# Attention scores from heads in place: two query tiles at once on halves or quarters of TensorE's array, without the moves that stacked high and low parts

## The chip, the cores and the metric

The kernel runs on one core of a Trainium2 chip. The core has five engines with queues of their own: TensorE (PE; its weight loads are shown apart as PEld), VectorE (DVE), ScalarE (ACT), GpSimd (POOL) and SyncE (SP), which here only issues DMAs. The metric is the device time of one execution in microseconds (us). Before the change the median of three runs is 1133.67 us (1133.57 to 1135.0); the execution that was profiled took 1130.16 us, and its profile spans 1128.2 us.

## The reference

Attention with a threshold, then a two-layer network with a quadratic gate:

```python
# q, k, v: 8 batches x 8 heads x 576 positions x 64, float32
scores = (1 / sqrt(64)) * q @ k^T
thresh = max(scores, axis=-1) - tau                  # tau = 0.02
scores = where(scores >= thresh, scores, -1e9)
attn = exp(scores - max(scores)); attn /= sum(attn) + 1e-9
x = (attn @ v), heads side by side                   # 4608 tokens x 512
h = x @ w_in                                         # 512 x 2048
g = where(h >= 1, h, where(h <= -1, 0, (h + 1)**2 / 4))
out = g @ w_out                                      # 2048 x 512
```

## The kernel before

**Numbers in two halves.** To keep nearly float32 precision on TensorE, every operand is scaled by a power of two and split into an fp16 high part and an fp16 low part (the rest). A product is made as high x high + low x high + high x low.

**Tiling.** The heads of a batch are taken as four pairs. A pair's q and k come from memory with the head dimension first, as 128 partitions: head 0 on partitions 0 to 63, head 1 on 64 to 127, 576 columns each. The queries of a pair are cut into two parts (256 and 320 positions; in batch 0 into three of 128, 128 and 320). A part consists of *tiles* of 128 query rows against all 576 keys. A full tile belongs to one head. The 320 positions leave 64 over for each head, and these make one *mixed* tile with head 0's rows on partitions 0 to 63 of the result and head 1's on 64 to 127. There are 288 tiles, 36 of them in batch 0.

**Scores.** A tile's scores go into one of two PSUM buffers `s` (two banks each, one for each half of the 576 keys). In batch 0 a full tile takes six matmuls on half of the array's rows (64 partitions of q and k, three products, two halves of the keys). In the batches after it the fp16 parts are first rearranged: ACT and DVE or POOL write them into `nat` (`hi` and `lo` in `add_qk`), and eight DMAs a pair (`move`, lines 591 to 596) copy them into `qq`, where a head's high part lies on partitions 0 to 63 and its low part on 64 to 127, and into `kk`, where each part of k lies on both halves. Then one matmul over 128 partitions makes (high + low) of q times one part of k, and a full tile takes four matmuls of 288 columns on the whole array. A mixed tile takes eight on half of its columns, two at a time.

**After the scores** (`add_tile`): DVE scales them and takes each row's minimum of the negated scores (`smax`, L994, and the threshold `sthr`, L998); ACT takes the exponential (`sexp`, L1001); DVE masks and sums (`smask`, L1015), which is the last reader of the buffer `s`; POOL normalizes (L1033), ACT and POOL split (L1038, L1041) into `hl`; SP sends it through a transposing DMA (L1063) into one of two buffers `eT`. When all tiles of a part are there, `add_av` multiplies with the transposed v (`av`, L1141, 28 matmuls on half of the columns each). Its result goes as high and low parts into `x`.

**The network.** For 256 tokens at a time, `ffn1` (L1213) makes 512 columns of h in `ph` with 24 or 48 matmuls; ACT and DVE apply the gate (L1219 to L1236); `ffn2` (L1258) adds to `acc`, 6 matmuls a step. The float64 weights are loaded, converted and split in the first 150 us.

**What sets the order.** The program is a list of operations (`plan.op`, with engine, planned duration, predecessors, buffers to take). A table of numbers, `ORDER`, gives the sequence in which `Plan.order` starts them; it gives each a planned time from the planned durations, `HOP` (handover between engines), `FREE`, `QUEUE`, `TURN` (PE's change between array shapes, told by an operation's `mode`), and each engine's instructions are issued sorted by it. Nothing is reordered at run time: each engine works through its list and waits where an operand or a buffer isn't ready. `take` names the rings of buffers: `s` (2), `ph` (3), `eT` (2), `hl` (3), `nat` (2), `kk` and `qq` (4 each).

Of the kernel before, what the change touches and what calls it, by code (L numbers as in the profile page):

```python
# [1319 lines left out]
```

## Time and profile before

| | |
|---|---|
| median of 3 runs | 1133.67 us |
| profiled execution | 1130.16 us |
| its span | 1128.2 us |
| mean granted TensorE clock | 0.987 |
| share of the 16 DMA engines taken by packets | 76.5% |
| share of the chain that ended last on PE | 70% |

A row of the timeline or of the groups gives the engine, the line, the operation, what it writes and reads, the part of the array that a matmul uses (`64*128` is 64 rows by 128 columns of the array), the shape of the moving operand, and how many. The ends of matmuls are modelled, so that neighbours overlap on paper; the time that a group really takes of PE is the start of the next row less its own, where nothing is noted as idle between.

### The profile page before, as it was taken

How to read it: one execution, taken by the hardware profiler on the slowest of the kernel's cores; microseconds unless marked ns; L12 is line 12 of the kernel's file. 1: busy time of each engine (PE TensorE's matmuls, PEld its weight loads, DVE VectorE, ACT ScalarE, POOL GpSimd, SP SyncE). 2: the span in 40 equal slices, each digit the busy share in tenths (PEclk: the TensorE clock that was granted, in tenths of full speed). 3: DMA queues.
4: the chain of work that ended last, by engine and by line, in shares of the span. 5: the costliest groups of instructions: out<-in, count | busy, mean ns of one | idle time of the engine just before them, and what ended most of it. 6: DMA issues, size and time to landing. Idle time of an engine off the chain costs nothing.

```text
span 1128.2 us, 26977 instructions
## 1 busy us (share of the span) xinstructions
PE 1088.4 (96%) x9396; PEld 756.9 (67%) x9396; DVE 892.0 (79%) x2704; ACT 868.7 (77%) x1676; POOL 790.2 (70%) x904
## 2 busy tenths in 40 slices
PE   4799999999999999999999999999999999999998
PEld 3456657766677676776777677676767677676674
DVE  5999889889689888899879898797679888785231
ACT  7989768779778788878877789777879877686352
POOL 6999997667766898678865986767787875655000
PEclk9799999999999999999999999999999999999999
DMA  9896899878968999669946999759796887554000
GB/s 332 345 208 143 148 207 189 145 142 185 206 125 148 200 193 228 135 134 198 216 96 114 182 203 195 122 106 200 163 197 140 171 157 133 105 103 97 19 11 20
DMA packets 435929, 179.40 MB, mean 159 GB/s; under 512 B 400464, under 2 KB 407632, under 8 KB 435792
## 3 DMA queue, kind: packets, MB, share of 16 engines
q1 hardware_dynamic: 435792, 177.67, 76.5%
q8 instruction: 74, 1.21, 0.4%
q14 instruction: 63, 0.52, 0.1%
HBM read 45.09 MB, written 9.44 MB: 48 GB/s over the span
## 4 chain that ended last, share of the span: by engine, by line
PE 70%; POOL 9%; DVE 8%; ACT 4%; DMA 4%; issue 4%; SPq 1%; DVEq 0%; POOLq 0%; ACTq 0%
PE acc L1258 27%; PE ph L1213 26%; PE s L977 9%; PE ph L1141 7%; POOL hl L1041 3%; DMA eT<-hl 2%; DVE s L994 2%; POOL e L1033 2%; DVE e L1015 2%; ACT e L1001 1%; DMA kk<-nat 1%; ACT hl L1038 1%; DMA WO<-in_moe_w_in_dram 1%; POOL raw L564 1%; SPq L594 0%
## 5 line engine op out<-in xcount | busy, mean ns | idle before, releaser
L1041 POOL TENSOR_TENSOR hl<-e,hl 128x576 f16<-128x576 f32 x285 | 366.6, 1292 | 115.8 <-ACT hl L1038 109.7
L1213 PE MATMUL ph<-x,WI 128*128 128x256 f16 (+1 forms) x4032 | 398.9, 257 | 1.5 <-DVE x L1153 0.7
L1213 PEld LDWEIGHTS <-WI 128*128 128x128 f16 x4032 | 346.3, 98 | 49.7 <-issue 5.8
L1033 POOL TENSOR_SCALAR e<-e,sm 128x576 f32<-128x576 f32 x285 | 219.1, 773 | 95.8 <-DVE sm L1025 62.2
L994 DVE TENSOR_SCALAR_CACHE_REDUCE s<-s,pc 128x576 f32<-128x576 f32 x288 | 232.7, 819 | 62.3 <-PE s L977 61.4
L1001 ACT ACTIVATE e<-s,sm 128x576 f32<-128x576 f32 x288 | 211.5, 741 | 62.5 <-DVE s L994 39.7
L1015 DVE SCALAR_TENSOR_TENSOR e<-s,sm,e 128x578 f32<-128x578 f32 x285 | 230.4, 815 | 33.1 <-ACT e L1001 28.6
L1038 ACT ACTIVATE hl<-e 128x576 f16<-128x576 f32 x285 | 193.1, 682 | 52.3 <-POOL e L1033 37.6
L1258 PE MATMUL acc<-WO,ga 128*128 128x512 f16 x864 | 202.3, 379 | 0.0
L977 PE MATMUL s<-kk,qq 128*128 128x288 f16 (+3 forms) x1360 | 190.5, 289 | 9.1 <-DVE e L1015 3.4
L977 PEld LDWEIGHTS <-qq 128*128 128x128 f16 (+3 forms) x1360 | 112.9, 100 | 71.8 <-issue 32.0
L1226 DVE SCALAR_TENSOR_TENSOR ph<-ph,fcs,asq 128x512 f32<-128x512 f32 (+1 forms) x160 | 112.0, 701 | 60.3 <-ACT asq L1222 59.1
L1219 ACT ACTIVATE asq<-ph,fcs 128x512 f32<-128x512 f32 (+1 forms) x160 | 115.6, 734 | 51.7 <-PE ph L1213 50.9
L1258 PEld LDWEIGHTS <-ga 128*128 128x128 f16 x864 | 82.5, 98 | 86.1 <-issue 2.4
L1141 PE MATMUL ph<-eT,vst 128*64 128x320 f16 (+2 forms) x1928 | 125.7, 282 | 7.5 <-DMA eT<-hl 2.3
L1141 PEld LDWEIGHTS <-vst 128*64 128x64 f16 x1928 | 100.8, 111 | 30.5 <-issue 20.5
L1236 DVE SCALAR_TENSOR_TENSOR ga<-ph,fcs,ga 128x256 f16<-128x256 f32 (+1 forms) x160 | 70.8, 451 | 29.7 <-ACT gb L1231 13.6
L1222 ACT ACTIVATE asq<-asq 128x512 f32<-128x512 f32 x144 | 90.8, 630 | 2.1
L1231 ACT ACTIVATE ga<-ph,fcs 128x256 f16<-128x256 f32 (+1 forms) x160 | 70.3, 451 | 27.8 <-DVE ph L1226 24.8
L1258 PE MATMUL acc<-WO,gb 128*128 128x512 f16 x300 | 72.8, 379 | 0.0
L1258 PE MATMUL acc<-WO,WI 128*128 128x512 f16 x288 | 67.2, 379 | 0.0
L1258 PE MATMUL acc<-WO 128*128 128x512 f16 x276 | 66.9, 379 | 0.0
(183 smaller groups left out, 1119.3 us busy)
## 6 DMA issues: line engine op xcount, KB each, us to landing
kk<-nat SPq DMA_DIRECT2D x112, 144.0 KB, 3.1
raw<-in_v_dram SPq DMA_DIRECT2D x32, 288.0 KB, 4.0
raw<-in_q_dram SPq DMA_DIRECT2D x32, 288.0 KB, 3.9
raw<-in_k_dram SPq DMA_DIRECT2D x32, 288.0 KB, 3.9
...
qq<-nat SPq DMA_DIRECT2D x112, 72.0 KB, 2.3
...
```

The costliest lines, as they stand in the source:

```text
L977: T.matmul(ap(s, s_ps)[r, f, :SH], q, k, start=ql == kl == 0, stop=kl == 1)
L994: V.tensor_scalar(sv(), sv(), c[:, 24 + v : 25 + v], None, ALU.mult, ALU.min, accum_out=t[:, 0:1])
L1001: A.activation(ev(), sv(), AF.Exp, bias=ap(m, sm)[:, 0:1], scale=-1.0)
L1015: V.scalar_tensor_tensor(ev(SH + 1), sv(SH + 1), t[:, 2:3], ev(SH + 1), ALU.is_le, ALU.mult, accum_out=t[:, 3:4])
L1033: G.tensor_scalar(ev(), ev(), ap(m, sm)[:, 5:6], ESC, ALU.mult, ALU.mult)
L1038: A.activation(part2(0), ev(), AF.Copy)
L1041: G.tensor_tensor(part2(w), ev(), part2(0), ALU.subtract)
L1141: T.matmul(o[hd * D : (hd + 1) * D, :n], vt[:, k, hd * D : (hd + 1) * D], t[:, kb, hd * n : (hd + 1) * n], start=m == 0, stop=m == len(blo ...
L1213: T.matmul(h[:, i], WTh["i"][:, u, wl * 512 + c * P : wl * 512 + (c + 1) * P], x[:, cc, xl, c0 : c0 + n].rearrange("p (t n) -> p t n", n=P ...
L1219: A.activation(tv()[:, :, c], hv()[:, :, c], AF.Relu, bias=fcs[:, b, q, 2 : 3], scale=fcs[:, b, q, 1 : 2])
L1226: V.scalar_tensor_tensor(hv()[:, :, c], hv()[:, :, c], fcs[:, b, q, 0 : 1], tv()[:, :, c], ALU.max, ALU.min)
L1258: T.matmul(ap(ab, accs), gv(h, gl)[:, x], WTh["o"][:, fc + i, wl * 512 : (wl + 1) * 512], start=fc + i == 0 and m == 0, stop=not left[0] a ...
```

## The change

**Scores of all batches are made from the natural rows.** `nat` and the `move` DMAs go; `hi` and `lo` write `qq` and `kk` directly, and a full tile takes six matmuls on half of the array's rows in every batch (three products, 64 partitions each).

**Two tiles at once.** For batches 1 to 7 a new function `score` makes two tiles in one operation: the full tile of head 0 on rows 0 to 63 of the array and that of head 1 on rows 64 to 127, matmul by matmul in turn, each into its own `s` buffer. Mixed tiles are made two at once too: that of an even pair and that of the next odd pair. In odd pairs the heads are swapped (`order_of`), so that the four 64-row, 64-column products fall on four different quarters of the array. This needs a fourth selector matrix (`sel`), four instead of three row scales in odd pairs, and swapped columns in `av`. Such an operation takes both `s` buffers at once.

**Other edits.** `eT` has three buffers instead of two. `ORDER` is new throughout, and so are the planner's numbers: handovers for each pair of engines, dearer PE operations in the first 66 us of the plan, some planned durations. CONV, SIGN and QHOW, which assign the work of conversion to engines, are unchanged.

```diff
-    nat = ring("nat", 2, [2, S], F16)
-    kk = ring("kk", 4, [2, 2, S], F16)
+    kk = ring("kk", 4, [2, S], F16)
...
-    eT = ring("eT", 2, [2 * SP // P, 2 * S1], F16)
+    eT = ring("eT", 3, [2 * SP // P, 2 * S1], F16)
...
-    sel = cp.tile([P, 3, P], BF16, name="sel")
+    sel = cp.tile([P, 4, P], BF16, name="sel")
...
+    def order_of(b, p):
+        return p % 2 if b else 0
...
         for c in range(0, n - r, P):
-            c2 = n + 2 * r * bool(r) + c if r else n + c
-            tiles += [(i, 0, [(0, q0 + c)], c), (i, 1, [(1, q0 + r + c)], n + r + c)]
+            if b:
+                together[len(tiles)] = together[len(tiles) + 1] = [len(tiles), len(tiles) + 1]
+            tiles += [(i, h0, [(h0, q0 + c)], c), (i, h1, [(h1, q0 + r + c)], n + r + c)]
         if r:
-            tiles.append((i, 2, [(0, q0 + n - r), (1, q0)], n - r))
+            if b:
+                both = together[first[i - 1] + 4] if p % 2 else []
+                both.append(len(tiles))
+                together[len(tiles)] = both
+            tiles.append((i, 2 + h0, [(h0, q0 + n - r), (h1, q0)], n - r))
...
-            for x in range(2):
-                for hd in range(2):
-                    def move(nb=nb, n=n, x=x, hd=hd):
...
+            done += [o2, o3]
...
+    def score(js):
+        own = []
+        for j in js:
+            i, v, heads, _ = tiles[j]
+            b, p = parts[i][:2]
+            own.append((plan.buf("s"), *QK[b, p][1:4], heads))
+
+        def qk():
+            for ql, kl in ((0, 0), (1, 0), (0, 1)):
+                for f in range(2):
+                    for s, qb, kb, _, heads in own:
+                        for x, (hd, c) in enumerate(heads):
+                            r = slice(0, P) if len(heads) == 1 else slice(x * D, (x + 1) * D)
+                            h = slice(hd * D, (hd + 1) * D)
+                            T.matmul(ap(s, s_ps)[r, f, :SH], ap(qb, qq)[h, ql, c : c + r.stop - r.start], ap(kb, kk)[h, kl, f * SH : (f + 1) * SH],
+                                     start=ql == kl == 0, stop=kl == 1)
...
+        o = plan.op("PE", cost, qk, [x for y in own for x in y[3]], take=[y[0] for y in own], uses=[x for y in own for x in y[1:3]], mode=2 + mixed)
...
-        s = plan.buf("s")
+        if j not in scored:
+            score(together.get(j, [j]))
+        s, scores = scored[j]
...
-                    T.matmul(o[hd * D : (hd + 1) * D, :n], vt[:, k, hd * D : (hd + 1) * D], t[:, kb, hd * n : (hd + 1) * n],
+                    x = hd ^ order_of(b, p)
+                    T.matmul(o[hd * D : (hd + 1) * D, :n], vt[:, k, hd * D : (hd + 1) * D], t[:, kb, x * n : (x + 1) * n],
```

**Where it moves instructions.** First PE, in the middle of the program, around one score group of the batches after batch 0. Before, an AV group (`L1141`) is followed by one tile, four matmuls into `s1`, and these by FFN matmuls:

```order
L1141 MATMUL ph0_63<-eT0_98,vst0_87 64x256
L977 LDWEIGHTS qq3_85
L977 MATMUL s1_62<-kk3_81,qq3_85 128x288
...
L1213 LDWEIGHTS WI_67
L1213 MATMUL ph2_65<-x1_104,WI_67 128x128
```

After the change, between two groups of FFN2 (`L1271`), whose full-array shape it breaks:

```order
L1271 MATMUL acc_66<-WO_68,ga0_107 128x512
L972 LDWEIGHTS qq3_83
L972 MATMUL s1_62<-kk3_79,qq3_83 128x288
L972 LDWEIGHTS qq3_83
L972 MATMUL s0_61<-kk3_79,qq3_83 128x288
...
L1271 LDWEIGHTS ga1_108
L1271 MATMUL acc_66<-WO_68,ga1_108 128x512
```

One operation now writes `s1` and `s0` in turn, 12 matmuls in all, where one tile with four matmuls stood.

Second, DVE, which reads and frees the `s` buffers, in the middle of the program. Before, a buffer's maximum (`L994`) and mask (`L1015`) often stand ahead of the other buffer's:

```order
L1015 SCALAR_TENSOR_TENSOR e0_91,sm3_125<-s1_62,sm3_125,e0_91 128x578
L1025 RECIPROCAL sm3_125<-sm3_125 128x1
L994 TENSOR_SCALAR s0_61,sm2_124<-s0_61,pc2_118 128x2x288
L998 TENSOR_SCALAR sm2_124<-sm2_124,tcs_140 128x1
L1226 SCALAR_TENSOR_TENSOR ph1_64<-ph1_64,fcs_147,asq0_100 128x512
L1015 SCALAR_TENSOR_TENSOR e1_92,sm2_124<-s0_61,sm2_124,e1_92 128x578
```

After the change (maximum `L1008`, mask `L1029`, an x part `L1166`, a v part `L646`), two pairs one after the other:

```order
L1008 TENSOR_SCALAR s1_62,sm2_123<-s1_62,pc1_116 128x2x288
L1012 TENSOR_SCALAR sm2_123<-sm2_123,tcs_139 128x1
L1008 TENSOR_SCALAR s0_61,sm1_122<-s0_61,pc1_116 128x2x288
L1029 SCALAR_TENSOR_TENSOR e3_92,sm2_123<-s1_62,sm2_123,e3_92 128x578
L1012 TENSOR_SCALAR sm1_122<-sm1_122,tcs_139 128x1
L1039 RECIPROCAL sm2_123<-sm2_123 128x1
L1039 RECIPROCAL sm5_126<-sm5_126 128x1
L1166 SCALAR_TENSOR_TENSOR x4_106<-ph0_63,x4_106 128x256
L1166 SCALAR_TENSOR_TENSOR x1_103<-ph0_63,x1_103 128x64
L929 TENSOR_SCALAR scs_145<-scs_145 128x2
L1029 SCALAR_TENSOR_TENSOR e1_90,sm1_122<-s0_61,sm1_122,e1_90 128x578
L646 SCALAR_TENSOR_TENSOR vb0_84<-raw2_71,scs_145,vb0_84 128x576
```

Both maxima now stand ahead of both masks, and PE can start the next pair only behind the second mask.

Third, SP's queue of DMAs, in the middle of the program. Before, `move` issues (`L594`, `L596`) stand between the transposes (`L1063`, `L651`) and the loads (`L530`, `L616`):

```order
L596 DMA qq0_82<-nat0_76 64x576 x2
L594 DMA kk0_78<-nat1_77 64x1152 x3
L1063 DMA_TRANSPOSE eT1_99<-hl2_97 128x9x128
L594 DMA kk0_78<-nat1_77 64x1152
L651 DMA_TRANSPOSE vst1_88<-vb0_86 128x14x128
L616 DMA raw0_69<-in_v_dram 128x576
```

After the change only the transposes (`L1077`, `L649`), loads (`L544`, `L614`) and stores are left, and the transposes go to three `eT` buffers:

```order
L1077 DMA_TRANSPOSE eT2_98<-hl0_93 128x9x128
L544 DMA raw4_73<-in_k_dram 128x576
L1077 DMA_TRANSPOSE eT0_96<-hl1_94 128x9x128
L544 DMA raw2_71<-in_q_dram 128x576
L1077 DMA_TRANSPOSE eT0_96<-hl2_95 128x9x128
L1077 DMA_TRANSPOSE eT1_97<-hl0_93 128x9x128
```

The 224 `move` issues are gone from the queue, 8 for each of 28 pairs of heads.

More of the change, by code (lines that the diff above doesn't have):

```diff
@@ L279 @@
 class Plan:
-    HOP = {"PE": 0.19, "DVE": 0.14, "ACT": 0.15, "POOL": 0.08, "SP": 0.06}
-    FREE, QUEUE, TURN = 0.16, 6.5, 0.097
+    ENG = ("PE", "DVE", "ACT", "POOL", "SP")
+    HOP = {
+        "PE": (0, 0.2, 0.2, 0.2, 0.2),
+        "DVE": (0.15, 0.165, 0.185, 0.22, 0.11),
+        "ACT": (0.16, 0.145, 0.125, 0.185, 0.13),
+        "POOL": (0.15, 0.08, 0.07, 0.06, 0.065),
+        "SP": (0.06, 0.08, 0.08, 0.075, 0.12),
+    }
+    FREE, QUEUE, TURN = 0.17, 6.0, 0.097
+    COLD = (66, 1.45)
     def __init__(self):
@@ L331, in order @@
             o.t = t
-            end = idle[o.eng] = t + o.cost + (self.TURN if o.eng == "PE" and o.mode != mode else 0.0)
+            end = t + o.cost
             if o.eng == "PE":
+                end = t + (self.TURN if o.mode != mode else 0.0)
+                end += o.cost * (self.COLD[1] if end < self.COLD[0] else 1)
                 mode = o.mode
+            idle[o.eng] = end
             if o.work:
@@ L345, in order @@
             for x in o.next:
-                x.t = max(x.t, end + (self.HOP[o.eng] if x.eng != o.eng else 0.0))
+                x.t = max(x.t, end + self.HOP[o.eng][self.ENG.index(x.eng)])
             for x in o.behind:
@@ L461, in consts @@
         G.memset(sel[D:, 2, D:], 1.0)
+        G.memset(sel[D:, 3, :D], 1.0)
+        G.memset(sel[:D, 3, D:], 1.0)
         G.memset(ones, 1.0)
@@ L481, in tau_consts @@
         V.tensor_scalar(tcs[:, 2:3], tau_sb, 0.0, None, ALU.max)
-    c_op = plan.op("POOL", 3.0, consts)
-    plan.op("ACT", 1.5, warm_up, [c_op])
+    c_op = plan.op("POOL", 5.2, consts)
+    plan.op("ACT", 0.24, warm_up, [c_op])
     t_ld = plan.op("SP", 0.45, lambda: Y.dma_start(tau_sb, tau.broadcast_to([P, 1])), work=LOAD)
-    t_op = plan.op("DVE", 0.2, tau_consts, [t_ld])
+    t_op = plan.op("DVE", 0.3, tau_consts, [t_ld])
+    def order_of(b, p):
+        return p % 2 if b else 0
     parts = []
@@ L491, in attn_ffn_kernel @@
         parts += [(b, p, q0, n) for q0, n in (CUT0 if not b else CUT) for p in range(NPAIR)]
-    tiles = []
+    tiles, together = [], {}
     first, last = {}, {}
@@ L541, in sums @@
         def sums():
-            o, c = stat(sb.slot, 6), cut(ap(cb, pc)[:, :2])
-            for v in range(3):
+            o, c = stat(sb.slot, 2 * nv), cut(ap(cb, pc)[:, :2])
+            for v in range(nv):
                 T.matmul(o[:, 2 * v : 2 * v + 2], sel[:, v], c, start=True, stop=True)
-        ps = plan.op("PE", 0.25, sums, [sq, sk], take=[sb], uses=[cb])
+        ps = plan.op("PE", 0.08, sums, [sq, sk], take=[sb], uses=[cb])
         def scales():
             c, t = ap(cb, pc), ph[sb.slot]
-            pow2(t[:, :6], t[:, 8:14], t[:, 16:22], c[:, 14:20])
-            V.tensor_scalar(c[:, 8:14], t[:, 16:22], 1.0, None, ALU.mult)
+            w = 2 * nv
+            pow2(t[:, :w], t[:, 8 : 8 + w], t[:, 16 : 16 + w], c[:, 16 : 16 + w])
+            V.tensor_scalar(c[:, 8 : 8 + w], t[:, 16 : 16 + w], 1.0, None, ALU.mult)
@@ L553, in scales2 @@
         def scales2():
             c = ap(cb, pc)
-            G.tensor_tensor(c[:, 20:22], c[:, 18:20], tcs[:, 0:2], ALU.mult)
+            G.tensor_tensor(c[:, 28:30], c[:, 20:22], tcs[:, 0:2], ALU.mult)
         so = plan.op("DVE", 0.56, scales, [ps, t_op], uses=[cb, sb])
-        sc1 = plan.op("POOL", 0.172, scales2, [so], uses=[cb])
-        sc2 = more_scales(cb, so)
+        sc1 = plan.op("POOL", 0.245, scales2, [so], uses=[cb])
+        sc2 = more_scales(cb, so, nv)
         done = []
-        for n, (rb, nb, ld) in enumerate(((rq, nq, lq), (rk, nk, lk))):
+        for n, (rb, nb) in enumerate(((rq, qb), (rk, kb))):
@@ L563, in norm, with hi @@
             def norm(rb=rb, n=n):
[L564 to L566 removed]
+                G.tensor_scalar(ap(rb, raw), ap(rb, raw), ap(cb, pc)[:, 28 + n : 29 + n], 1.0, ALU.mult, ALU.mult)
+            def hi(how, rb=rb, n=n):
                 if how == "D":
[L568 removed]
+                    A.activation(parts(n)[:, 0], ap(rb, raw), AF.Copy, scale=ap(cb, pc)[:, 28 + n : 29 + n])
@@ L584, in add_qk @@
             o2, o3 = plan.join(o2), plan.join(o3)
-            if not b:
-                done += [o2, o3]
-                continue
-            o = None
-            for x in range(2):
-                for hd in range(2):
-                    def move(nb=nb, n=n, x=x, hd=hd):
-                        src = ap(nb, nat)[hd * D : (hd + 1) * D]
-                        if n:
-                            Y.dma_start(ap(kb, kk)[x * D : (x + 1) * D, hd], src)
-                        else:
-                            Y.dma_start(ap(qb, qq)[x * D : (x + 1) * D, hd], src[:, x])
-                    mine = kb if n else qb
-                    w = KMOVE if n else QMOVE
-                    o = plan.op("SP", 0.63, move, [o2, o3 if n or x else o2],
-                                take=[mine] if x == hd == 0 else [], uses=[nb, mine], work=w, behind=o)
-                    done.append(o)
+            done += [o2, o3]
         QK[b, p] = cb, qb, kb, done, sc2
@@ L619, in ssq @@
                 A.activation(junk, ap(rb, raw), AF.Square, accum_out=vssq[:, b, p : p + 1])
-            l = plan.op("SP", 0.53, load, take=[rb], work=LOAD)
+            l = plan.op("SP", 0.53, load, take=[rb], work=LOAD if b else (1.2, 1.2, 1.9))
             squares.append(plan.op("ACT", 0.67, ssq, [l], uses=[rb]))
@@ L801, in add_w @@
                     o1 = plan.op("ACT", 0.561, fixed, [l], **for_pb)
-                    o2 = plan.op("POOL", 0.66, lowed, [l])
+                    o2 = plan.op("POOL", 0.705, lowed, [l])
                 else:
@@ L884, in add_w @@
                     if how == "D":
-                        done.append(plan.op("DVE", 1.3, rest2, [o]))
+                        done.append(plan.op("DVE", 0.88, rest2, [o]))
                         read.append(done[-1])
@@ L955, in attn_ffn_kernel @@
     begun, prev = {}, {}
+    scored = {}
+    def score(js):
[13 more added lines that the diff above has]
+                                     start=ql == kl == 0, stop=kl == 1)
+        mixed = v >= 2
+        cost = (0.735, 0.76)[mixed] + 0.01 * (len(js) - 1)
+        o = plan.op("PE", cost, qk, [x for y in own for x in y[3]], take=[y[0] for y in own], uses=[x for y in own for x in y[1:3]], mode=2 + mixed)
+        for j, y in zip(js, own):
+            scored[j] = y[0], o
     def add_tile(j):
@@ L965, in add_tile @@
             part_tr[i] = []
-        def qk():
-            for ql, kl in ((0, 0), (1, 0), (0, 1)) if not b else ((0, 0), (0, 1)):
-                for f in range(2):
-                    for hd, c in heads:
-                        r = slice(0, P) if len(heads) == 1 else slice(hd * D, (hd + 1) * D)
-                        n = r.stop - r.start
-                        h = slice(hd * D, (hd + 1) * D)
-                        q = ap(qb, qq)[h, ql, c : c + n] if not b else ap(qb, qq)[:, hd, c : c + n]
-                        k = ap(kb, kk)[h, 0, kl, f * SH : (f + 1) * SH] if not b else ap(kb, kk)[:, hd, kl, f * SH : (f + 1) * SH]
-                        T.matmul(ap(s, s_ps)[r, f, :SH], q, k, start=ql == kl == 0, stop=kl == 1)
         def sv(w=SH):
@@ L1063, in send @@
             Y.dma_start_transpose(ap(eTb[i], eT)[:, : 2 * w // P, col : col + P], ap(x, hl)[:, : 2 * w])
-        cost = (0.492, 0.522) if b else (0.735, 0.76)
-        o = plan.op("PE", cost[v // 2], qk, ready, take=[s], uses=[qb, kb], mode=v // 2 + (0 if b else 2))
-        o = plan.op("DVE", 0.739, smax, [o, c2], take=[m], uses=[s, cb])
+        o = plan.op("DVE", 0.739, smax, [scores, c2], take=[m], uses=[s, cb])
         o2 = plan.op("DVE", 0.128, sthr, [o], uses=[m])
```

48 lines of the change are left out of this document (23 added, 25 removed), and 429 rows, old and new, of the table ORDER.

## The prediction

> **What bounds the kernel now.** I read the profile's page first: its busy line, its slices, and the chain that ended last.
>
> ```profile
> span 1128.2 us, 26977 instructions
> PE 1088.4 (96%) x9396; PEld 756.9 (67%) x9396; DVE 892.0 (79%) x2704; ACT 868.7 (77%) x1676; POOL 790.2 (70%) x904
> PE 70%; POOL 9%; DVE 8%; ACT 4%; DMA 4%; issue 4%; SPq 1%; DVEq 0%; POOLq 0%; ACTq 0%
> PE acc L1258 27%; PE ph L1213 26%; PE s L977 9%; PE ph L1141 7%; POOL hl L1041 3%; DMA eT<-hl 2%; DVE s L994 2%; POOL e L1033 2%; DVE e L1015 2%; ACT e L1001 1%; DMA kk<-nat 1%; ACT hl L1038 1%; DMA WO<-in_moe_w_in_dram 1%; POOL raw L564 1%; SPq L594 0%
> ```
>
> TensorE (PE) is busy for 96% and carries 70% of the chain. A busy share with modelled ends could hide gaps, so the second view is the busy time by stretches, and the third the timeline of PE, where the start of one group and the start of the next give its true length.
>
> ```profile
> core 0: us, PE busy (x) PEld busy (x) DVE busy (x) ACT busy (x) POOL busy (x), PEclk, DMA share, GB/s
> 0.00:20.00 20.00, 9.12 (x61) 7.25 (x62) 8.25 (x33) 12.75 (x29) 9.73 (x42) 1.00 0.90 321
> 20.00:60.00 40.00, 29.05 (x184) 17.32 (x184) 38.03 (x126) 37.03 (x72) 38.02 (x56) 0.72 0.95 328
> 60.00:150.00 90.00, 83.84 (x974) 57.91 (x972) 79.98 (x248) 76.06 (x146) 85.35 (x99) 0.97 0.87 172
> 150.00:300.00 150.00, 143.87 (x1176) 98.84 (x1174) 126.34 (x380) 120.80 (x231) 113.26 (x126) 1.00 0.89 175
> 300.00:500.00 200.00, 199.77 (x1772) 143.35 (x1771) 173.67 (x537) 163.72 (x320) 151.39 (x161) 1.00 0.87 168
> ...
> 900.00:1100.00 200.00, 200.00 (x1673) 141.25 (x1672) 130.52 (x371) 129.07 (x235) 88.49 (x87) 1.00 0.48 90
> ```
>
> ```profile
> 599.96 2.84 PE L1213 MATMUL ph<-x,WI 128*128 128x128 f16 x48
> 602.63 0.65 PE L977 MATMUL s<-kk,qq 128*128 128x288 f16 x4
> 603.12 2.84 PE L1213 MATMUL ph<-x,WI 128*128 128x128 f16 x48
> 605.90 0.68 PE L977 MATMUL s<-kk,qq 128*64 128x288 f16 x8
> 606.51 0.18 PE L625 MATMUL ph<-vssq,ones 128*128 128x4 bf16 x1
> 606.55 1.46 PE L1258 MATMUL acc<-WO,ga 128*128 128x512 f16 x6
> 607.84 0.65 PE L977 MATMUL s<-kk,qq 128*128 128x288 f16 x4
> 608.33 1.46 PE L1258 MATMUL acc<-WO,ga 128*128 128x512 f16 x6
> 609.72 2.09 PE L1141 MATMUL ph<-eT,vst 128*64 128x320 f16 x28
> 611.75 0.66 PE L977 MATMUL s<-kk,qq 128*128 128x288 f16 x4
> ...
> 623.71 0.22 PE L544 MATMUL ph<-pc,sel 128*128 128x2 bf16 x3
> 623.78 1.46 PE L1258 MATMUL acc<-WO,WI 128*128 128x512 f16 x6
> ```
>
> From 300 us on PE never stands still (200.00 busy of 200): every row starts where the one before has streamed its columns. Six 512-column matmuls take 607.84 - 606.55 = 1.29 us, 0.215 each. So from there on the time is the sum of PE's work, and what PE is spared counts in full. PE's gaps lie earlier: 10.9 us before 20, 10.9 from 20 to 60, 6.2 from 60 to 150 (POOL busy 85.35 of 90), 6.1 from 150 to 300.
>
> **What the change removes and adds on PE.** How many tiles there are follows from the code and the counts:
>
> ```profile
> L977 PE MATMUL s<-kk,qq 128*128 128x288 f16 x896 | 140.2, 286 | 4.0 <-DVE e L1015 2.7 <-DMA kk<-nat 0.9
> L977 PE MATMUL s<-kk,qq 64*128 64x288 f16 x192 | 28.3, 298 | 5.0 <-DVE vst L684 3.2 <-DVE eT L1091 0.9 <-DVE e L1015 0.7
> L977 PE MATMUL s<-kk,qq 128*64 128x288 f16 x224 | 19.0, 291 | 0.1
> ```
>
> Batches 1 to 7 have 896 / 4 = 224 full tiles and 224 / 8 = 28 mixed ones. A full tile now costs 603.12 - 602.63 = 0.49 us (also 608.33 - 607.84); four matmuls, 0.1225 each. A mixed tile costs 606.51 - 605.90 = 0.61, with one change of the array's shape in it. That change costs about 0.10: from FFN matmuls to a 128*64 group it took 609.72 - 608.33 = 1.39 where six such matmuls alone take 1.29. So the mixed tile itself is 0.51. Together 224 x 0.49 + 28 x 0.51 = **124.0 us**.
>
> The new form already runs in batch 0, one tile at a time:
>
> ```profile
> 71.45 0.89 PE L977 MATMUL s<-kk,qq 64*128 64x288 f16 x6 [0.24 <-DVE e L1015]
> 72.28 0.40 PE L790 MATMUL acc<-WO 128*128 128x128 bf16 x4
> ...
> 76.92 1.17 PE L977 MATMUL s<-kk,qq 64*128 64x288 f16 x12
> 78.03 0.63 PE L790 MATMUL acc<-WO 128*128 128x128 bf16 x8
> ...
> 88.92 1.59 PE L977 MATMUL s<-kk,qq 64*128 64x288 f16 x12
> ...
> 96.06 1.76 PE L977 MATMUL s<-kk,qq 64*128 64x288 f16 x18
> 97.75 0.45 PE L1213 MATMUL ph<-x,WI 128*128 128x128 f16 x5
> ```
>
> One tile on half of the rows takes 72.28 - 71.45 = 0.83 with a shape change behind it, 0.73 alone. Two tiles on the two halves, written one after the other, took 78.03 - 76.92 = 1.11, or 1.01 without the change. Serial they would be 1.46, and the row at 88.92, where the second started late, shows that case (1.59 to its end). So the halves do run side by side, and since the order of batch 0 lets the second tile start behind two matmuls of the first, 1.01 is an upper bound. The change interleaves the two tiles matmul by matmul; that is shown for quarters only: the row at 96.06 is one half-array tile (0.73), a change, a mixed tile of 12 interleaved quarter matmuls, and a change, in 1.69. That leaves 0.76 for the 12, against 0.73 for six alone. I take 0.75 for a pair of full tiles (bounds 0.73 and 1.01) and 0.77 for a pair of mixed ones, whose four quarters at once no row shows (bounds 0.76 and 1.52, two in series). 112 x 0.75 + 14 x 0.77 = **94.8 us**. Spared: 29.2.
>
> **The shape changes eat more than half of it.** A full tile had the shape of the FFN's matmuls; a pair has not. Counted over the whole order, PE changes shape 196 times before and 370 times after. 174 x 0.10 = **17.4 us** back. A selector matmul more for each odd pair of heads: 14 x 0.02 ((623.78 - 623.71) / 3) = 0.3. Net: 124.0 - 94.8 - 17.4 - 0.3 = **11.5 us less on PE**.
>
> The price of a shape change is the term to doubt; its rival is below.
>
> **What goes besides.** The moves:
>
> ```profile
> DMA packets 435929, 179.40 MB, mean 159 GB/s; under 512 B 400464, under 2 KB 407632, under 8 KB 435792
> ...
> L1141 PE MATMUL ph<-eT,vst 128*64 128x320 f16 (+2 forms) x1928 | 125.7, 282 | 7.5 <-DMA eT<-hl 2.3
> ...
> kk<-nat SPq DMA_DIRECT2D x112, 144.0 KB, 3.1
> ...
> qq<-nat SPq DMA_DIRECT2D x112, 72.0 KB, 2.3
> ```
>
> 224 issues leave SP's queue and 112 x (144 + 72) KB = 24 MB of 179 leave the DMA engines. They hide now: PE's own wait for them is the 0.9 us above. I count nothing, with 0 to 10 us kept for the range (a rival below). ACT, DVE and POOL keep their instructions, but for wider scale rows of nanoseconds and POOL's two more memsets at the start. The third eT buffer lets a part's transposes begin before the last but one has been multiplied; PE waits for those transposes 2.3 us in all today, so it hides too. The order is new everywhere; I take it to keep PE as full as today, and give its failure to the second rival.
>
> **Sum.** The profiled run took 1130.16, 1.96 beyond its span: 1130.16 - 11.5 = 1118.7. The median of the runs shown, 1133.67, lies 3.5 above the profiled one, and I forecast against it: 1133.67 - 11.5 = **1122**. The score groups that fall before 150 us, where POOL is the fuller engine, may save nothing: batch 1's share, 18 of 126 pairs, 1.6 us.
>
> **Rivals.**
>
> *The early gaps close too.* One seventh of the moves, 3.5 MB, belongs to batch 1 and falls into the time when the DMA engines are 0.87 to 0.95 busy; at 328 GB/s that is 10.5 us of transfers. For it: PE has 12.3 us of gaps between 60 and 300. Against it: DVE, ACT and POOL are 93 to 95% busy from 20 to 60 and keep all their work. Half of the gaps gives 1116, all of it 1110.
>
> *Pairs starve PE (slower).* A pair takes both score buffers at once, so the next pair waits until DVE has masked both tiles; before, one buffer was filled while the other was worked on.
>
> ```profile
> 507.51 0.83 DVE L994 TENSOR_SCALAR_CACHE_REDUCE s<-s,pc 128x576 f32<-128x576 f32 x1 [0.19 <-PE s L977]
> 508.25 0.14 DVE L994 DVE_READ_ACCUMULATOR s<-s,pc 128x1 f32 x1
> 508.25 0.82 DVE L994 TENSOR_SCALAR_CACHE_REDUCE s<-s,pc 128x576 f32<-128x576 f32 x1
> 508.99 0.14 DVE L994 DVE_READ_ACCUMULATOR s<-s,pc 128x1 f32 x1
> ...
> L1015 DVE SCALAR_TENSOR_TENSOR e<-s,sm,e 128x578 f32<-128x578 f32 x285 | 230.4, 815 | 33.1 <-ACT e L1001 28.6
> L1001 ACT ACTIVATE e<-s,sm 128x576 f32<-128x576 f32 x288 | 211.5, 741 | 62.5 <-DVE s L994 39.7 <-DVE sm L1025 12.4 <-POOL hl L1041 3.6
> ```
>
> The chain is a handover (0.19), two maxima 0.74 apart, two masks of at most 0.82, and a handover: 0.2 + 1.48 + 1.64 + 0.2 = 3.5 us if DVE does nothing between; ACT's exp of the second tile (0.74) fits beside the first mask. In the new order the PE work that stands between two pairs of batches 1 to 7 is at least 4.1 us by the durations above (mostly 24 FFN1 matmuls of 256 columns, each taken at twice the (602.63 - 599.96) / 48 = 0.056 of 128 columns, and 12 FFN2: 5.2), so it covers the chain with 0.6 to 1.7 us to spare for what DVE has queued between, such as an x part or a gate of 0.7. It decides at 11.5 / 126 = 0.09 us of stall per pair; at 0.25 us it costs 31 and the kernel takes 1154. The margin speaks against it, DVE's 79% for it.
>
> *Shape changes cost more.* Leaving a half-array group at 72.28 and a full one at 609.72 cost about 0.10 each, but the groups of the new form that follow AV or stand before it are few in this trace. At (29.2 - 0.3) / 174 = 0.17 the change wins nothing: 1134. The rows of batch 0 speak against it. The Trainium skill, TensorEngine Tiling (Array Packing), Key Properties, says that changing the tiling mode drains the engine, and TensorE: Matmul & The Clock Gate, Single matmul latency, gives a warm matmul a constant of 398 cycles at 2.4 GHz beside its columns. A drain that costs all of it would be 0.166 (an estimate from that page), and 174 of them 28.9; the rows here show 0.10.
>
> *The tiles overlap only in part (the change doesn't do what it says).* At the bound 1.01 for each of 126 pairs: 127.3 + 17.4 + 0.3 - 124.0 = 21 more, 1155; wholly serial (1.46 and 1.52), 184.8: 1212. Row 76.92 and the quarters speak against both. The Trainium skill, TensorE: Matmul & The Clock Gate, Measured speedup vs the span model, has four row tiles 3.07 times as fast as one after the other. That share, 77%, would make a pair 0.95 (an estimate from that page), near the bound; the quarters at 96.06 show 0.76.
>
> **How the numbers follow.** My forecast, PE-bound with unchanged gaps, 1115 to 1129: 0.68. Early gaps close, 1105 to 1115: 0.14. Pairs starve PE, 1129 to 1160: 0.13, of which 0.02 still faster, 0.03 the same, 0.08 slower. Dear shape changes, about 1134: 0.02, the same. Partial overlap, 1150 and more: 0.03. The range 1108 to 1135 leaves out some 0.04 below and 0.11 above. A measurement of this kernel tells about 0.2% (2.3 us) from no change. Faster by more: 0.68 + 0.14 + 0.02 = 0.84; same 0.03 + 0.02 = 0.05; slower 0.08 + 0.03 = 0.11.
>
> **What would show it.** In the new trace a pair's 12 matmuls should stand 0.85 us ahead of the next group's start (0.75 and a change), 24 quarters 0.87; the stretches from 300 to 1080 should still show PE 200 of 200. Gaps of PE before the score group, ended by DVE's mask, would be the second rival; 1.1 us for 12 the third; fuller PE rows between 60 and 300 the first. The forecast is wrong if shape changes into quarter or half arrays cost more than 0.10, or if the new order leaves PE waiting for FFN operands.

## The result, and the profile after

The changed kernel took 1122.94 us (median of 4 runs, 1121.39 to 1124.7), the kernel before 1134.34 in the same comparison (4 runs, 1133.57 to 1136.76): a ratio of 0.9896, 95% interval 0.9872 to 0.9921. A second comparison, with which the experiments below are compared, gave this:

> The changed kernel as it is, beside the kernel before on the chip of these runs: 11.5 us faster, ratio 0.990, by the sum of PE's work.

Measured: 1122.63 us (1122.3 to 1123.29), ratio 0.9902 [0.9887, 0.9917], which is 11 us less than before. The forecast was 1122.

The page of the changed kernel, in the lines that were shown of the kernel before (the span, busy time by engine, the DMA total, the chain that ended last by engine):

```profile
span 1122.6 us, 27608 instructions
PE 1079.2 (96%) x9970; PEld 722.9 (64%) x9970; DVE 899.7 (80%) x2704; ACT 865.9 (77%) x1676; POOL 788.9 (70%) x906
DMA packets 418008, 154.63 MB, mean 138 GB/s; under 512 B 396880, under 2 KB 396880, under 8 KB 417872
PE 67%; DVE 9%; DMA 8%; POOL 6%; ACT 5%; issue 4%; SPq 1%; POOLq 0%; DVEq 0%; ACTq 0%
```

PE is still the bound and still 96% busy. But its share of the chain fell from 70 to 67% and DMA's rose from 4 to 8%: PE has begun to wait for others. The busy time by stretches shows where (the columns are those of the prediction's table: the stretch, its length, busy time and instructions of PE, PEld, DVE, ACT and POOL, then PE's clock, DMA share and GB/s). First the changed kernel:

```profile
0.00:20.00 20.00, 9.94 (x51) 7.95 (x51) 6.94 (x24) 11.98 (x27) 9.31 (x43) 1.00 0.92 326
20.00:60.00 40.00, 27.01 (x190) 16.97 (x190) 37.97 (x125) 35.51 (x69) 37.73 (x56) 0.79 1.02 343
60.00:150.00 90.00, 80.89 (x917) 54.73 (x915) 82.57 (x254) 78.29 (x150) 84.20 (x100) 0.94 0.78 149
150.00:300.00 150.00, 148.08 (x1363) 98.26 (x1361) 133.27 (x401) 124.77 (x236) 113.90 (x126) 1.00 0.72 135
300.00:500.00 200.00, 197.77 (x1872) 134.23 (x1873) 171.57 (x517) 161.89 (x317) 152.41 (x164) 1.00 0.74 144
500.00:700.00 200.00, 197.92 (x1871) 132.76 (x1868) 173.82 (x521) 160.33 (x314) 153.91 (x168) 1.00 0.72 140
700.00:900.00 200.00, 199.78 (x1867) 133.06 (x1866) 158.83 (x484) 158.50 (x312) 143.81 (x159) 1.00 0.67 133
900.00:1100.00 200.00, 200.00 (x1737) 135.57 (x1735) 128.67 (x366) 128.95 (x242) 93.64 (x95) 1.00 0.44 82
```

PE's gaps before 300 us are what they were: 10.1 + 13.0 + 9.1 + 1.9 = 34.1, against 10.9 + 10.9 + 6.2 + 6.1 = 34.1. From 300 to 900 there are now 2.2 + 2.1 + 0.2 = 4.5 us, where the kernel before had about 1: 0.23 in its row from 300 in the prediction, and in its two next ones

```profile
500.00:700.00 200.00, 199.27 (x1729) 140.61 (x1727) 170.54 (x508) 162.20 (x321) 154.00 (x170) 1.00 0.87 173
700.00:900.00 200.00, 200.00 (x1695) 138.45 (x1695) 159.27 (x494) 159.19 (x308) 150.01 (x170) 1.00 0.78 157
```

The changed kernel's timeline of PE from 598 to 640 us gives the length of a pair, from its start to the next row's start:

```profile
601.29 0.93 PE L972 MATMUL s<-kk,qq 64*64 64x288 f16 x24
602.15 2.76 PE L1271 MATMUL acc<-WO,ga 128*128 128x512 f16 x12
...
606.22 1.09 PE L972 MATMUL s<-kk,qq 64*128 64x288 f16 x12
607.24 2.85 PE L1226 MATMUL ph<-x,WI 128*128 128x128 f16 x48
...
614.01 0.91 PE L972 MATMUL s<-kk,qq 64*128 64x288 f16 x12
614.85 2.85 PE L1226 MATMUL ph<-x,WI 128*128 128x128 f16 x48
...
618.93 2.09 PE L1154 MATMUL ph<-eT,vst 128*64 128x320 f16 x28
620.96 0.91 PE L972 MATMUL s<-kk,qq 64*128 64x288 f16 x12
621.79 2.76 PE L1271 MATMUL acc<-WO,WI 128*128 128x512 f16 x12
```

A pair on halves takes 614.85 - 614.01 = 0.84 with one shape change (0.83 at 620.96), a pair on quarters 602.15 - 601.29 = 0.86; 0.85 and 0.87 were forecast. The pair at 606.22 took 1.02: its second tile's first matmul started 0.195 us after the first tile's, where most pairs have 0.003. The mask of its buffer ended only at 606.36, and the matmul started at 606.41. After 300 us nine of 103 pairs were held in their middle like this, 2.7 us in all by the starts in the trace; the rows count most of that as busy.

The list of waits has the releasers (the columns are total, times, longest). Over the whole span, the first two lines are PE's score matmuls waiting for DVE's mask, in the kernel before and in the changed one. The third is ACT, which waits longer than before (13.7 us) for the transposes that free its `hl` buffers:

```profile
PE s L977 <- DVE e L1015: 3.4, 8, 0.8
PE s L972 <- DVE e L1029: 6.1, 8, 1.8
ACT hl L1052 <- DMA eT<-hl: 28.0, 32, 2.5
```

Between 300 and 1100 us the mask ends only 1.0 of the changed kernel's 4.5 us of gaps. The rest stands ahead of the network's matmuls, which wait for ACT to empty `acc` (L1289), for DVE's part of the gate (L1249), or for less:

```profile
PE acc L1271 <- ACT ob L1289: 1.4, 1, 1.4
PE s L972 <- DVE e L1029: 1.0, 2, 0.8
PE ph L1226 <- DVE WO L1249: 0.9, 1, 0.9
```

### The profile page after: what moved, and what is told of

Same layout as the page of the kernel before. It is cut to its first block, busy times and chain, and to the rows that moved or that the text cites. A ratio compares the mean times of both kernels' runs of the same rounds, so it can differ in the third digit from the quotient of the medians.

```text
span 1122.6 us, 27608 instructions
## 1 busy us (share of the span) xinstructions
PE 1079.2 (96%) x9970; PEld 722.9 (64%) x9970; DVE 899.7 (80%) x2704; ACT 865.9 (77%) x1676; POOL 788.9 (70%) x906
## 4 chain that ended last, share of the span: by engine, by line
PE 67%; DVE 9%; DMA 8%; POOL 6%; ACT 5%; issue 4%; SPq 1%; POOLq 0%; DVEq 0%; ACTq 0%
PE acc L1271 26%; PE ph L1226 25%; PE ph L1154 8%; PE s L972 7%; DMA eT<-hl 5%; POOL hl L1055 3%; DVE s L1008 3%; DMA WO<-in_moe_w_in_dram 2%; DVE e L1029 2%; POOL e L1047 2%; ACT hl L1052 1%; ACT e L1015 1%; DMA vst<-vb 1%; DVE vb L646 1%; ACT junk L550 0%
## 5 line engine op out<-in xcount | busy, mean ns | idle before, releaser
L1008 DVE TENSOR_SCALAR_CACHE_REDUCE s<-s,pc 128x576 f32<-128x576 f32 x288 | 230.1, 819 | 49.2 <-PE s L972 46.4
L1029 DVE SCALAR_TENSOR_TENSOR e<-s,sm,e 128x578 f32<-128x578 f32 x285 | 229.7, 815 | 35.0 <-ACT e L1015 27.5
L1015 ACT ACTIVATE e<-s,sm 128x576 f32<-128x576 f32 x288 | 209.9, 741 | 55.6 <-DVE s L1008 36.9
L1271 PE MATMUL acc<-WO,ga 128*128 128x512 f16 x864 | 203.7, 380 | 1.4 <-ACT ob L1289 1.4
L972 PE MATMUL s<-kk,qq 64*128 64x288 f16 (+1 forms) x1920 | 147.7, 285 | 7.2 <-DVE e L1029 6.1
L1271 PEld LDWEIGHTS <-ga 128*128 128x128 f16 x864 | 79.3, 98 | 93.1 <-issue 13.2
L972 PEld LDWEIGHTS <-qq 64*128 64x128 f16 (+1 forms) x1920 | 84.1, 97 | 68.9 <-issue 44.3
L1249 DVE SCALAR_TENSOR_TENSOR ga<-ph,fcs,ga 128x256 f16<-128x256 f32 (+1 forms) x160 | 70.6, 450 | 27.6 <-ACT WO L1244 10.3
L1271 PE MATMUL acc<-WO,gb 128*128 128x512 f16 x300 | 72.0, 379 | 0.0
L1271 PE MATMUL acc<-WO,WI 128*128 128x512 f16 x294 | 70.6, 379 | 0.0
L1271 PE MATMUL acc<-WO 128*128 128x512 f16 x270 | 64.7, 379 | 0.0
(181 smaller groups left out, 1120.7 us busy)
```

Source lines behind the costliest of these rows:

```text
L972: T.matmul(ap(s, s_ps)[r, f, :SH], ap(qb, qq)[h, ql, c : c + r.stop - r.start], ap(kb, kk)[h, kl, f * SH : (f + 1) * SH], start=ql == kl = ...
L1008: V.tensor_scalar(sv(), sv(), c[:, 24 + v : 25 + v], None, ALU.mult, ALU.min, accum_out=t[:, 0:1])
L1015: A.activation(ev(), sv(), AF.Exp, bias=ap(m, sm)[:, 0:1], scale=-1.0)
L1029: V.scalar_tensor_tensor(ev(SH + 1), sv(SH + 1), t[:, 2:3], ev(SH + 1), ALU.is_le, ALU.mult, accum_out=t[:, 3:4])
L1271: T.matmul(ap(ab, accs), gv(h, gl)[:, x], WTh["o"][:, fc + i, wl * 512 : (wl + 1) * 512], start=fc + i == 0 and m == 0, stop=not left[0] a ...
```

## The experiments

"Over the change" below is the difference of a run's ratio from 0.9902, times 1134 us. Every ratio is to the kernel before on the same chip; the experiments e1 to e6, e8, e9 and e12 are edits of the changed kernel, e7 and e10 of the kernel before.

### What a pair is worth: do two tiles really run side by side?

**One tile of a pair written out before the other.** The loop over the tiles moves outwards:

```diff
-            for ql, kl in ((0, 0), (1, 0), (0, 1)):
-                for f in range(2):
-                    for s, qb, kb, _, heads in own:
+            for s, qb, kb, _, heads in own:
+                for ql, kl in ((0, 0), (1, 0), (0, 1)):
+                    for f in range(2):
```

> The changed kernel, but a pair's matmuls are written tile by tile (all of the first, then all of the second) instead of in turn. Theory (the gain comes from two tiles running side by side on a PE that bounds the kernel): as in batch 0 before, the second tile starts two matmuls behind the first, so a pair takes 1.01 us instead of 0.745: 126 x 0.27 = 33 us more than the changed kernel, about 1156, some 2% over the kernel before. Rival (the gain comes from the moves that went, or from the new order): at most 5 us more than the changed kernel.

Measured: 1147.35 us, ratio 1.0117 [1.0095, 1.0139], 24 over the change. Its timeline of PE:

```profile
602.51 1.17 PE L972 MATMUL s<-kk,qq 64*128 64x288 f16 x12
603.61 3.25 PE L1154 MATMUL ph<-eT,vst 128*64 128x256 f16 x56
```

The pair takes 603.61 - 602.51 = 1.10, 1.00 without the change of shape: the 1.01 that the prediction read from batch 0 as its upper bound. So the interleaving alone is worth 0.26 us on each of 126 pairs, 33 in all, and with one tile written behind the other the change would have lost. Even so the tiles overlap, since two in series would take 1.46. In the trace's records the matmul that waits for the second tile's buffer starts 0.265 us after the pair's first one, ahead of three matmuls of the first tile that stand before it in the program; in batch 0 of the kernel before (the row at 76.92 in the prediction) it is the same. So it is not the order of batch 0 that lets the second tile start early, as the prediction has it, and by these recorded starts "Nothing is reordered at run time" does not hold for matmuls on different halves. That 24 and not 33 came out has its reason in the same kernel's stretches:

```profile
300.00:500.00 200.00, 199.71 (x1827) 136.17 (x1826) 167.48 (x501) 158.82 (x311) 148.74 (x161) 1.00 0.74 143
500.00:700.00 200.00, 200.00 (x1816) 135.55 (x1815) 169.35 (x516) 156.89 (x306) 152.23 (x167) 1.00 0.72 138
```

PE is full again there: the slower pairs give DVE the time that it lacked, and about 4 of the 9 us are the gaps of 300 to 700 us that went. No pair is held in its middle any more either, where the change loses 3.6 us after 150 us, 1.0 of it in those gaps. The other 2 to 3 us are not accounted for.

**The natural rows without the pairs.** The kernel before with its old order, without moves and stacking, all three products as six half-array matmuls a tile, one tile at a time (`kk` and `qq` with six buffers each):

```diff
-            for ql, kl in ((0, 0), (1, 0), (0, 1)) if not b else ((0, 0), (0, 1)):
+            for ql, kl in ((0, 0), (1, 0), (0, 1)):
...
-                        q = ap(qb, qq)[h, ql, c : c + n] if not b else ap(qb, qq)[:, hd, c : c + n]
+                        q = ap(qb, qq)[h, ql, c : c + n]
```

> The kernel before, in its own order, with scores from the natural rows one tile at a time and no moves (kk and qq have six buffers instead of four, nat goes): the change without two tiles at once. PE changes shape 527 times instead of 196. Theory: 224 x (0.73 - 0.49) + 28 x (0.76 - 0.51) + 331 x 0.097 = 93 us more than the kernel before, less up to 27 where two tiles stand side by side in the order and overlap in part: 66 to 93 more, 1200 to 1227. Rival (the moves were what cost): as fast as the kernel before or faster.

Measured: 1203.71 us, ratio 1.0625 [1.0607, 1.0642]: 71 over the kernel before. Natural rows one tile at a time are a heavy loss; 331 more shape changes in an order that was not made for them would be 33 us of it at 0.10 each. Together with e1 it says that the gain hangs on two tiles at once.

### The price of a shape change

**One change more in each pair** (the last of the three products on quarters, the first two on halves). Its control, **all three products on quarters**, is the same edit without `and kl == 1`: small matmuls, but no further change of shape.

```diff
                     for s, qb, kb, _, heads in own:
+                        if len(own) == 2 and len(heads) == 1 and kl == 1:
+                            heads = [(heads[0][0], heads[0][1]), (heads[0][0], heads[0][1] + D)]
```

> The changed kernel, but the last of the three products of each full pair (112) is made on quarters of the array: the same columns, one more change of shape for each pair. Theory (a change costs 0.10 us of PE's time, and PE bounds): 112 x 0.10 = 11 us more than the changed kernel, 13 with the first quarter matmul's extra 0.02. Rival (a change is hidden): 0 to 2 us. Rival (a change costs a whole drain, 0.166): 19 us.

> The changed kernel, but all three products of each full pair are made on quarters: 24 matmuls instead of 12, no more changes of shape. It is the control of the run with one more change. Theory: four quarters at once take as long as two halves, 112 x 0.02 = 2 us more than the changed kernel at most. If twice the matmuls and weight loads cost 0.1 us a pair: 11 us more, and the run with one more change then says nothing on the change alone.

Measured: with the change more, 1134.37 us, ratio 1.0000 [0.9987, 1.0013], 11 over; the control 1125.67, 0.9931 [0.9909, 0.9953], 3 over, of which its interval leaves 1 to 6. One pair in the timeline of PE, in the first fence of the kernel with one more change, in the second of the control:

```profile
617.11 1.03 PE L974 MATMUL s<-kk,qq 64*128 64x288 f16 x16
618.07 2.85 PE L1228 MATMUL ph<-x,WI 128*128 128x128 f16 x48
```

```profile
614.00 0.93 PE L974 MATMUL s<-kk,qq 64*64 64x288 f16 x24
614.87 2.85 PE L1228 MATMUL ph<-x,WI 128*128 128x128 f16 x48
```

0.96 against 0.87 for quarters throughout and 0.84 for halves throughout: two thirds halves and one third quarters would be 0.85, so the change inside costs 0.11. By the totals it is (11 - 3) / 112 = 0.07 if the whole cost of quarters is taken off, and (11 - 1) / 112 = 0.09 if a third of it is. The 0.10 of the prediction stands; 0.17, from which the change would have won nothing, does not.

### How close the next bound is

**Slower masks**: a further DVE instruction ahead of the mask of each pair's second tile, 0.26 us of work on a scratch tile:

```diff
+            if b and j == together[j][1]:
+                V.tensor_scalar(slow, slow, 1.0, None, ALU.mult)
```

> The changed kernel with one more DVE instruction of about 0.26 us (190 columns of float32, onto themselves) ahead of the mask of each pair's second tile, so that both score buffers come free that much later: 126 x 0.26 = 33 us of DVE. Theory (the PE work between two pairs covers DVE's chain with 0.6 to 1.7 us to spare): 3 to 12 us more than the changed kernel, where the cover is short. Rival (pairs already wait for DVE): 25 to 33 us more.

Measured: 1134.44 us, ratio 1.0007 [0.9995, 1.002], 12 over the change, the top of the first expectation. The group of the score matmuls (busy, mean ns of one, idle time ahead of them and what ended it), in the first fence of the changed kernel, in the second of this one:

```profile
L972 PE MATMUL s<-kk,qq 64*128 64x288 f16 (+1 forms) x1920 | 147.7, 285 | 7.2 <-DVE e L1029 6.1
```

```profile
L973 PE MATMUL s<-kk,qq 64*128 64x288 f16 (+1 forms) x1920 | 154.8, 286 | 14.0 <-DVE e L1032 12.4 <-DVE vst L683 0.9
```

Of 33 us put on DVE, 12 came through. Waits for the mask grew by 6, and the group's busy time by 7, since it holds the waits inside a pair (as at 606.22 above).

**Less work for PE**: batches 1 to 7 without one of the three products.

```diff
-            for ql, kl in ((0, 0), (1, 0), (0, 1)):
+            for ql, kl in ((0, 0), (1, 0), (0, 1)) if len(own) == 1 else ((0, 0), (0, 1)):
```

> The changed kernel without the product of q's low part with k's high part in batches 1 to 7 (8 matmuls a full pair, 16 a mixed one), so its scores there lack that part. Theory (PE bounds even after the change): 126 x 0.245 = 31 us less than the changed kernel, about 1092. Rival (DVE at 80% or the score buffers bind next): 10 to 20 us less only, and PE's rows from 300 to 900 show it idle.

Measured: 1108.4 us, ratio 0.9781 [0.9766, 0.9795]: 14 less than the change, of 31 that PE was spared. Its stretches:

```profile
300.00:500.00 200.00, 194.95 (x1775) 129.55 (x1775) 172.57 (x520) 163.86 (x325) 152.37 (x165) 1.00 0.74 143
500.00:700.00 200.00, 195.42 (x1774) 130.93 (x1773) 174.01 (x526) 163.08 (x319) 153.66 (x167) 1.00 0.74 145
700.00:900.00 200.00, 198.66 (x1772) 132.44 (x1770) 166.00 (x509) 161.96 (x320) 151.60 (x169) 1.00 0.66 130
900.00:1100.00 200.00, 197.31 (x1632) 129.19 (x1631) 119.80 (x334) 119.47 (x229) 78.27 (x78) 1.00 0.42 78
```

5.1 + 4.6 + 1.3 + 2.7 = 13.7 us of gaps, where the change has 4.5. So 9 of the 17 us that did not arrive are new gaps after 300 us. Of the rest, 5 never left PE's busy time, which fell by 26 (1079.2 to 1052.9) and not by 31: after 300 us 25 pairs are now held in their middle for 10.3 us, where the change has nine and 2.7, and much of that counts as busy. The last 3 are not accounted for. PE is still the bound after the change, but what it is spared from here on counts for half.

### The moves

**The kernel before without its moves** (those of batches 2 to 7, 192 of 224):

```diff
                     def move(nb=nb, n=n, x=x, hd=hd):
+                        if at >= 8:
+                            return
```

> The kernel before, in its own order, without the moves of batches 2 to 7 (192 of 224; the scores there use the q and k that batch 1 left in the buffers). Theory (the moves were hidden behind a PE that never waits): within 3 us of the kernel before. Rival (the moves cost the kernel before part of what the change gained): 5 us or more faster than the kernel before.

Measured: 1132.58 us, ratio 0.9989 [0.9976, 1.0002]: at most 3 us. These moves were hidden in the kernel before, as the prediction had it; batch 1's 32 stayed.

**As many moves put into the changed kernel**, as copies of q and k to unused HBM (the moves had stayed in SBUF), one behind each of a pair of heads' first eight transposes in SP's queue:

```diff
             Y.dma_start_transpose(ap(eTb[i], eT)[:, : 2 * w // P, col : col + P], ap(x, hl)[:, : 2 * w])
+            if b and moved[b, p] < 8:
...
+                if n:
+                    Y.dma_start(aside[1, hd, to], ap(QK[b, p][2], kk)[h])
+                else:
+                    Y.dma_start(aside[0, hd, to, 0], ap(QK[b, p][1], qq)[h, y])
```

> The changed kernel with DMAs of the size and number of the old moves put back: 8 a pair of heads for batches 1 to 7, from qq and kk into memory that nobody reads (HBM, since SBUF is full), one behind each of the first 8 transposes of a pair. Theory (the moves were hidden): 0 to 3 us more than the changed kernel. Rival (part of the gain is the DMA engines' and SP's relief): 5 to 11 us more.

Measured: 1157.15 us, ratio 1.019 [1.0157, 1.0223], 33 over the change. Neither expectation held. Three runs took the cost apart: the same 224 issues with 4 KB each, the same bytes in 84 issues, and the small issues again with a constant tile as their source.

```diff
-                    Y.dma_start(aside[1, hd, to], ap(QK[b, p][2], kk)[h])
+                    Y.dma_start(aside[1, hd, to, 0, :32], ap(QK[b, p][2], kk)[h, 0, :32])
```

> As the run with the moves put back (34 us more than the changed kernel, which nothing I had named gives), same 224 issues at the same places on SP's queue, but each moves 64 x 32 values only. If the issues cost (they stand between the transposes and hold SP's queue): 20 to 34 us more than the changed kernel. If the bytes cost (24 MB more for the DMA engines, written to HBM): 0 to 8 us more.

```diff
+                if moved[b, p] in (2, 4, 7):
+                    Y.dma_start(aside[moved[b, p] // 4, moved[b, p] % 2], ap(QK[b, p][1 + (moved[b, p] > 2)], kk if moved[b, p] > 2 else qq))
```

> As the run with the moves put back, the same bytes in 3 issues a pair of heads instead of 8, each over all 128 partitions. If the issues cost: 3/8 of 34, 10 to 15 us more than the changed kernel. If the bytes cost: 28 to 36 us more.

```diff
+    still = cp.tile([P, 32], F16, name="still")
...
+                Y.dma_start(aside[n, hd, to, 0, :32], still[h])
```

> The same 224 issues of 4 KB in the same places of SP's queue as in e8_small_moves, but they read a constant tile, so that they hold neither q nor k buffers and wait for nothing. Theory (the slot in SP's queue costs, 0.6 us of it for each issue, between a tile's transposes): as in e8, 23 to 33 us over the change, 1146 to 1156. Rival (the copies keep the q and k buffers taken for longer, so that the transposes of the next q and k come late): 0 to 6 us, 1122 to 1129. In between: both.

Measured:

| 224 copies' worth as | us | ratio | over the change |
|---|---|---|---|
| 224 issues, 24 MB (e4) | 1157.15 | 1.019 [1.0157, 1.0223] | 33 |
| 224 issues, 0.9 MB (e8) | 1151.55 | 1.0138 [1.0096, 1.018] | 27 |
| 84 issues, 24 MB (e9) | 1133.84 | 1.0002 [0.9993, 1.0012] | 11 |
| 224 issues, 0.9 MB, constant source (e12) | 1139.6 | 1.004 [1.0024, 1.0057] | 16 |

A part of this is the clock. In the trace of e8, TensorE's granted clock (the third number from the end) is below 1.00 in three stretches after 150 us in which the changed kernel has 1.00:

```profile
150.00:300.00 150.00, 142.42 (x1303) 94.60 (x1302) 125.80 (x382) 116.31 (x222) 106.79 (x119) 0.98 0.73 132
300.00:500.00 200.00, 192.39 (x1782) 128.43 (x1781) 164.81 (x489) 152.97 (x300) 142.86 (x153) 0.98 0.74 137
500.00:700.00 200.00, 195.76 (x1811) 129.74 (x1809) 167.93 (x514) 160.02 (x314) 154.12 (x171) 0.99 0.70 136
```

That is 3 + 4 + 2 = 9 us of clock. Three of the four runs of e8 and of e4 have a mean clock of 0.979 to 0.981; the fourth of e8, at 0.986, took 1141.97 us, 19 over the change, and the fourth of e4, at 0.988, 1150.48 us, 27 over (each against the kernel before on its chip). All ten of e9 had 0.983 or more. Why the clock fell is not shown.

The bytes cost little: 6 us for 24 MB by the medians of e4 and e8, within the two intervals, and 8 by their two runs at the higher clock, one each. The count costs more: 0.09 us an issue in e8 by the run at 0.986, 0.12 by the median, and 0.13 in e9, bytes included. Most of it remains when the copies hold no q or k buffer and wait for none (16 by the median of e12, 15 by that of its five runs at 0.985 or more). What then remains is their place in SP's queue. SP's queue in e12 (start, length, what it issued):

```profile
616.03 1.33 SPq L1080 DMA_TRANSPOSE eT<-hl  x1
617.45 0.54 SPq L1085 DMA_DIRECT2D aside<-still  x1
618.04 1.37 SPq L1080 DMA_TRANSPOSE eT<-hl  x1
619.47 0.58 SPq L1085 DMA_DIRECT2D aside<-still  x1
620.15 1.32 SPq L1080 DMA_TRANSPOSE eT<-hl  x1
```

A transpose occupies the queue for 1.3 us and a copy, however small, for 0.6, so transposes with a copy between them follow each other every 2.0 to 2.1 us. Who is made late at the end is PE. Its busy time from 150 to 1100 us (one stretch of 950 us), of the changed kernel, e8, e9 and e12 in this order:

```profile
150.00:1100.00 950.00, 943.55 (x8701) 633.88 (x8700) 766.17 (x2286) 734.45 (x1419) 657.66 (x709) 1.00 0.65 126
```

```profile
150.00:1100.00 950.00, 925.79 (x8426) 617.32 (x8425) 758.47 (x2267) 720.44 (x1387) 656.75 (x709) 0.99 0.68 128
```

```profile
150.00:1100.00 950.00, 935.82 (x8614) 628.70 (x8611) 763.05 (x2278) 726.24 (x1400) 655.97 (x708) 1.00 0.74 152
```

```profile
150.00:1100.00 950.00, 933.87 (x8558) 625.18 (x8558) 763.28 (x2277) 726.80 (x1400) 657.24 (x709) 1.00 0.68 128
```

The gaps, 950 less the first busy time, are 6.5, 24.2, 14.2 and 16.1 us: 17.7, 7.7 and 9.6 above the change, some two thirds of the 27, 11 and 16; in e8 the 9 us of clock make up the rest. The waits of e8 name the releasers:

```profile
PE s L974 <- DVE e L1031: 16.8, 21, 3.0
ACT hl L1054 <- DMA eT<-hl: 35.0, 34, 3.2
```

PE waits 11 us longer than in the changed kernel for DVE's mask, and ACT 7 longer for `hl` buffers that the transposes free. The way from the queue to PE would be: late transposes, late `hl` buffers, ACT held there with its next exp behind, and the mask that needs exp late. It is argued, not shown: ACT's wait is as long or longer in e9 (38.9) and e12 (37.4), which lose less. The 11 us by which e8 lies above e12 are in part clock as well (9 us in e8's trace after 150 us, against 2 in that of e12, which has 0.99 from 500 to 700). What is left for the q and k buffers as the source is 4 us by the runs at the higher clock and 8 by the gaps of the two traces, through their later release or through the copies' own waiting; neither was tried alone. Nor was the third `eT` buffer, or the new order, taken alone.

## Why the prediction was right

**PE's time bounds the kernel: right.** e1, e2 and e7 put work on PE and the time followed (24 of 33, 11 of an expected 11 to 13, 71 of an expected 66 to 93). Beyond the change it holds by half only, as e5 shows (14 of 31).

**29.2 us of score time spared: right.** By the medians from a group's start to the next, a full tile takes 0.490 and a mixed one 0.514 before, a pair 0.841 and one of mixed tiles 0.862 after, each of these two with a change of 0.096: 224 x 0.490 + 28 x 0.514 - 112 x 0.745 - 14 x 0.766 = 30.0. *The tiles overlap only in part* falls: e1 is that case, built, and it was slower than before. The Trainium skill (TensorE: Matmul & The Clock Gate, Measured speedup vs the span model) has 3.07 for four row tiles, from which the estimate of 0.95 a pair came; that share does not carry over to these two tiles: 0.74 is all but a full factor of two over 1.46.

**17.4 us given back by shape changes: right.** PE changes shape 196 and 370 times in the two traces too. A 512-column matmul takes 0.216 us (median) before another of its shape and 0.312 before a half-array group, so that a change costs 0.096 and 174 of them 16.7; e2 with its control put the single one at 0.07 to 0.11. *Shape changes cost more*, at 0.17, falls. That changing the tiling mode drains the engine, as the Trainium skill has it (TensorEngine Tiling (Array Packing), Key Properties), agrees with there being a price; the estimate of 0.166 for it does not, as 112 such changes would have put e2 19 us or more over the change and not 11.

**The moves count nothing: right for what was asked, by a fact that was not seen.** e10 shows that they were hidden in the old order. In the new one, e4 and e8 show, such issues are not hidden where they were put, one behind a transpose. That an order made with them in mind could hide them again isn't excluded. So to count them at nothing was the right term of the sum, while "no gain from the moves" would be a wrong summary of the change.

***The early gaps close too*: did not happen.** 34.1 us of gaps before 300 us stayed 34.1, though the transfers there fell from 175 to 135 GB/s between 150 and 300; the gap only moved, from that stretch into those before it. e10 does not test this rival, since it leaves the moves of batch 1 where they were.

***Pairs starve PE*: happened, but small, and waits are the term that the sum left out.** That the stretches from 300 to 1080 would still show PE 200 of 200 was wrong: 4.5 us of gaps stand there, 3.5 more than the 1.0 of before. DVE's mask, which this rival named, ends only 1.0 us of them; with the waits inside pairs that count as busy it cost 2.7. Most of the other gaps are what the prediction's last sentence names, PE waiting for the network's operands and buffers in the new order. Nine pairs after 300 us were held, not 103: the work between two pairs covered the chain nearly always. e6 shows the margin: 0.26 us more in DVE's chain costs 0.09 a pair, so the price that would have cancelled the gain (0.09 a pair) lies only that far away.

**The sum.** The terms as measured give -30.0 + 16.7 + 0.3 = -13.0 us, with the waits (3.5 of gaps, 1.6 more inside pairs) -7.9, where the medians differ by 11. The profiled executions differ by 5.6 in their spans (1128.2 and 1122.6): PE's busy time fell by 9.2 (1088.4 to 1079.2), and the gaps after 300 us grew by 3.5. With the profile of the second comparison, whose span is 1120.7, it is 7.5. The profiled execution of the kernel before (1130.16 us) lies below all four runs of the comparison (1133.57 to 1136.76), and that of the changed kernel (1124.7) is the slowest of its four. So the steps are each shown to within a microsecond or two, but the total only to within about 3; that the forecast met the median within 1 us is in part luck, since the waits were not in it.
